# The second product of the second MLP with weights stationary, and its results turned on VectorE

## The chip, the cores and the metric

The kernel runs on one core of one Trainium2 chip. A core has TensorE (PE, whose weight loads are shown apart as PEld), VectorE (DVE), ScalarE (ACT), GpSimd (POOL), SyncE (SP, which here only issues DMAs) and 16 DMA engines. The metric is device time in microseconds, the median of some executions; smaller is better.

## The reference

Attention without softmax, then two MLPs one behind the other, all in float32:

```
scores = q @ k^T / 8, times gamma_h ** (i - j) where i >= j, else 0     # 4 x 8 heads, 576 tokens, 64 dims
x  = (scores @ v) as 2304 tokens x 512
h  = max(x @ w_in, 0);           x1  = (h * h) @ w_out                  # first MLP,  512 -> 2048 -> 512
h2 = x1 @ w_in2;  g = h2 * clip(h2 + 3, 0, 6) / 6;  out = g @ w_out2    # second MLP, 512 -> 2048 -> 512
```

The change touches only the last product, `g @ w_out2`, and the stores of `out`.

## The kernel before

Float32 products are made of three passes on rounded parts: an operand is split into a high part and a low part, and high x high, high x low and low x high are added up in PSUM. Attention and the first MLP come first and fill the span up to about 483 us; they write x1 to HBM. Meanwhile the second MLP's weights are narrowed, combined and split, and stored to HBM as `w_in_hl` and `w_out_hl`.

The second MLP then runs in three supers of 768 tokens. Each of its two products is done block-wise, with seven block products in place of eight: both operands are cut in 2 x 2 blocks, so a block has 384 tokens (`HALF`) and half of the features. `ORDER = (1, 6, 7, 5, 2, 4, 3)` is the order of the seven. In each super there are two stages:

- *First stage* (line 977): for each of 8 `j` and each of the 7 products, 6 matmuls with 128 columns of weights stationary and 384 tokens moving: 336 matmuls. ACT, DVE and POOL make the inputs `aop` of the second stage of what comes out.
- *Second stage* (lines 1017 to 1040): for each of the 7 products `q` and each of 8 `k`, the input is split by `a_cast` (ACT, line 921) and `a_low` (DVE, line 925) into one of 6 `spl` tiles. Then come 9 matmuls (line 1026): 128 tokens of `spl` stationary (3 groups), 256 columns of `w_out_hl` moving (`HALFD`), 3 passes. That is 504 matmuls. Two PSUM banks `z` hold the result of a product, tokens on partitions: two groups of tokens in one bank (512 wide), the third in the other (256 wide).

After products 1, 6 and 7, `merge` (lines 932 to 939) adds the banks to the running sums `held`. After products 5, 2, 4 and 3, `emit` (lines 941 to 953) makes output blocks in `tmp` tiles (four buffers), by DVE or, for product 2, by ACT, and SP stores each of the two pieces with one DMA, in runs of 256 floats (1 KB).

The weights of both stages come through a ring of 7 tiles of 512 KB (`ring_load`, lines 770 to 781): one tile serves two `k`. SP issues the load of tile n + 7 when PE has finished with tile n, so SP waits for PE before most ring loads. SP's queue is in order: a ring load behind a store waits until the store is issued. A store also waits until the DMA eight before it has landed, since eight semaphores are used in turn. A `tmp` tile is written again only when the store that read it has landed.

The order of the instructions on each engine is set when the program is built: a heap holds the work of ACT, DVE, POOL and SP with a due time (`at`), and `run(now)` issues what is due before the next group of matmuls. `t_in` and `t_out` are the planned times of a product in the first stage and in the second. An `spl` tile is planned to be written as soon as an older one is free.

Of the kernel before, what the change touches and what calls it, by code (L numbers as in the profile page):

```python
# [10 lines left out]
F32 = mybir.dt.float32  # L11
# [4 lines left out]
AF = mybir.ActivationFunctionType  # L16
ALU = mybir.AluOpType

P = 128
# [12 lines left out]


SUPERS, HALF = 3, 384
NTT = HALF // P
NJ = NF // 2
HALFD = DM // 2

# [55 lines left out]
def retention_moe_kernel(ctx: ExitStack, tc, qk, kv, w1, w2, cst, out):  # L94
# [5 lines left out]
    nc = tc.nc  # L100
    nblk = len(BLOCKS)
    start = np.concatenate([[0], np.cumsum([n for n, _ in BLOCKS])]).tolist()
# [658 lines left out]
    half = len(steps) - NJ  # L761
# [123 lines left out]
            at(t, ring_load, n)  # L885

    t_in = 6 * (HALF + 32) / 2400.0
    t_out = 3 * NJ * NTT * (HALFD + 32) / 2400.0
    now = 0.0
    act = nc.scalar.activation  # L890
    tt = nc.vector.tensor_tensor
# [32 lines left out]
        t = splits[s, q, k]  # L924
        tt(t[:, 1, :], f32(q, k), t[:, 0, :].bitcast(F32), ALU.subtract)  # L925

    PIECES = ((0, 2), (2, 1))

    def piece(t, n):
        return t[:, n * HALFD :] if n == 2 else t[:, : 2 * HALFD]  # L930

    def merge(q, o, u):

        for b, (n, m) in zip(A_BANKS[q], PIECES):
            p = z[b][:, : m * HALFD]
            if u is None:
                act(piece(o, n), p, AF.Copy, 0.0, SIXTH)
            else:
                stt(piece(o, n), p, SIXTH, piece(u, n), ALU.mult, ALU.add)

    def emit(s, q, half, od, u):
        for b, (n, m) in zip(A_BANKS[q], PIECES):
            t = tmpp.tile([P, 512], F32, tag="tmp", name=f"o_{s}_{q}_{n}")[:, : m * HALFD]
            p = z[b][:, : m * HALFD]
            if u is None:
                act(t, p, AF.Copy, 0.0, SIXTH)
            else:
                stt(t, p, SIXTH, piece(u, n), ALU.mult, ALU.add)
            t0 = (2 * s + half) * HALF + n * P
            dst = out[t0 : t0 + m * P, HALFD * od : HALFD * (od + 1)]  # L950
            nc.sync.dma_start(
                dst.rearrange("(n p) d -> p n d", p=P), t.rearrange("p (n d) -> p n d", n=m)
            )

    for s in range(SUPERS):
        t_a = now + NJ * 7 * t_in

        for m, (q, k) in enumerate((q, k) for q in ORDER for k in range(NJ)):
            free = t_a + (m - NSPL + 1) * t_out / NJ
            if m < NSPL:  # L960
                free = max(free, now + (k + 1) * 7 * t_in + 1.0)
            at(free + 0.1, a_cast, s, q, k)
            at(free + 0.7, a_low, s, q, k)
        for j in range(NJ):
            e = j % 2
            bank = {q: z[k][:, :HALF] for q, k in H_BANK[e].items()}
            s1, u2 = held[2 * e][:, 0, :], held[2 * e][:, 1, :]
            u3 = held[1][:, e, :]
            c22, c21, c12 = s1, u3, u2
            for i, q in enumerate(ORDER):  # L970
                run(now)
                w = wring[s, 0, j, i // 2][:, i % 2]
                x = x_ops[q]
                for k, (u, wi, xi) in enumerate(
                    [(u, wi, xi) for wi, xi in ((0, 0), (1, 0), (0, 1)) for u in range(2)]
                ):
                    nc.tensor.matmul(  # L977
                        bank[q],
                        w[:, wi, u * P : (u + 1) * P],
                        x[:, u, xi, :],  # L980
                        start=k == 0 and q not in (2, 4, 3),
                        stop=k == 5,
                        skip_group_check=q in (2, 4, 3),
                    )
                now += t_in
                if i % 2 or i == 6:
                    ring_done(now + 0.1)
                if q == 1:
                    at(now, act, s1, bank[1], AF.Copy)
                elif q == 6:  # L990
                    at(now, tt, u2, bank[6], s1, ALU.add)
                elif q == 7:
                    at(now, tt, u3, bank[7], u2, ALU.add)
                elif q == 5:
                    at(now, tt, c22, bank[5], u3, ALU.add)
                    at(now + 0.8, relu3, 4, j, c22)
                    at(now + 1.3, gate, 4, j, c22)
                elif q == 2:
                    at(now, relu3, 1, j, bank[1])
                    at(now + 0.75, gate, 1, j, bank[1])  # L1000
                elif q == 4:
                    at(now, tt, c21, bank[4], u2, ALU.add)
                    at(now + 0.8, relu3, 2, j, c21)
                    at(now + 1.3, gate, 2, j, c21)
                else:
                    at(now, tt, c12, bank[3], u2, ALU.add)
                    at(now + 0.8, relu3, 7, j, c12)
                    at(now + 1.3, gate, 7, j, c12)
                    at(now + 2.0, pool_op, 5, 7, 4, ALU.add, j)
                    at(now + 2.1, pool_op, 7, 1, 7, ALU.subtract, j)  # L1010
                    at(now + 2.2, pool_op, 6, 5, 1, ALU.subtract, j)
                    at(now + 2.3, pool_op, 3, 2, 6, ALU.subtract, j)
        if s + 1 < SUPERS:
            for u, st in enumerate(x_stages(s + 1)):
                for k, part in enumerate(st):
                    at(now + 1.0 + 25.0 * u * (k > 0) + 3.0 * k + 4.0 * (k > 0), do, part)
        s1, u3, u2 = [held[k].rearrange("p a b -> p (a b)")[:, : NTT * HALFD] for k in range(3)]
        for i, q in enumerate(ORDER):
            for k in range(NJ):
                run(now)  # L1020
                w, sp = wring[s, 1, q, k // 2], splits[s, q, k]
                for n in range(NTT):
                    rows = slice(P * n, P * (n + 1))
                    o = z[A_BANKS[q][n // 2]][:, HALFD * (n % 2) : HALFD * (n % 2 + 1)]
                    for m, (g, wi) in enumerate(((0, 0), (0, 1), (1, 0))):
                        nc.tensor.matmul(  # L1026
                            o,
                            sp[:, g, rows],
                            w[:, k % 2, wi, :],
                            start=k == 0 and m == 0 and n % 2 == 0 and q not in (2, 4, 3),  # L1030
                            stop=k == NJ - 1 and m == 2 and n > 0,
                            skip_group_check=q in (2, 4, 3),
                        )
                now += t_out / NJ
                if k % 2:
                    ring_done(now + 0.1)
            if q in (1, 6, 7):
                at(now, merge, q, *{1: (s1, None), 6: (u2, s1), 7: (u3, u2)}[q])
            else:
                at(now, emit, s, q, *{2: (0, 0, None), 5: (1, 1, u3), 4: (1, 0, u2), 3: (0, 1, u2)}[q])  # L1040
# [38 lines left out]
```

## Time and profile before

| | |
|---|---|
| time, median of 3 runs | 843.64 us (843.55 to 847.52) |
| the profiled execution's own time | 844.25 us |
| its span, first to last instruction | 842.4 us |
| PE busy | 823.3 us, 98% of the span |
| PEld busy | 758.6 us, 90% |
| DVE busy | 578.1 us, 69% |
| ACT busy | 385.7 us, 46% |
| POOL busy | 203.9 us, 24% |
| DMA packets | 136843, 185.79 MB, mean 221 GB/s |
| granted TensorE clock | 1.000 (2.4 GHz) |

Busy time is the time in which an engine had at least one instruction under way. The span leaves out what lies around the program: 844.25 - 842.4 = 1.85 us.

### The profile page before, as it was taken

The numbers are of one execution on the slowest core, as the hardware profiler recorded it, in microseconds if no ns is written. First come the engines' busy times: TensorE is split into PE (matmuls) and PEld (weight loads), VectorE is DVE, ScalarE is ACT, GpSimd is POOL, SyncE is SP. The second block draws the span as 40 slices with busy tenths as digits, with TensorE's granted clock in tenths as the row PEclk, the third lists the DMA queues.
The fourth block names the chain that finished last, engine by engine and source line by source line (L and its number), as shares of the span: only waits on it lengthen the run. The fifth ranks groups of instructions, "written<-read, shape, count | busy, mean of one in ns | idle before, by whom it ended". The sixth has DMA issues, their size and how long they took to land.

```text
span 842.4 us, 15782 instructions
## 1 busy us (share of the span) xinstructions
PE 823.3 (98%) x6052; PEld 758.6 (90%) x6052; DVE 578.1 (69%) x1034; ACT 385.7 (46%) x710; POOL 203.9 (24%) x182
## 2 busy tenths in 40 slices
PE   8899999998999999989999999999999999999998
PEld 7778779998888889989888899999999999999997
DVE  5788886565655556666546977887576987577763
ACT  1756644443434344434434633566333656234542
POOL 3366462001110101110000045520055500256300
PEclk9999999999999999999999999999999999999999
DMA  8927505666765457665547797788888978877773
GB/s 327 343 95 270 172 4 146 176 195 174 225 188 164 143 162 213 186 180 169 155 137 239 213 340 255 268 329 264 277 252 259 337 256 277 272 249 262 261 257 129
DMA packets 136843, 185.79 MB, mean 221 GB/s; under 512 B 7360, under 2 KB 94016, under 8 KB 136768
## 3 DMA queue, kind: packets, MB, share of 16 engines
q1 hardware_dynamic: 136768, 184.79, 68.7%
q8 instruction: 48, 0.79, 0.4%
q14 instruction: 27, 0.22, 0.1%
HBM read 145.96 MB, written 38.80 MB: 219 GB/s over the span
## 4 chain that ended last, share of the span: by engine, by line
PE 77%; DMA 6%; issue 5%; DVE 5%; POOL 3%; ACT 2%; SPq 2%; DVEq 0%; POOLq 0%; ACTq 0%
PE z L1026 21%; PE z L977 21%; PE acc L508 16%; PE h L472 16%; DMA w_in_hl<-seven 3%; POOL w L177 2%; DMA raw<-w_dram 1%; PE o L444 1%; PE o L434 1%; DVE r L482 1%; DMA w_out_hl<-seven 1%; ACT g L484 1%; DVE seven L568 1%; POOL q L333 1%; SPq L221 1%
## 5 line engine op out<-in xcount | busy, mean ns | idle before, releaser
L508 PE MATMUL acc<-g,w 128*128 128x512 f32 (+1 forms) x960 | 216.0, 373 | 3.0 <-ACT g L484 2.8
L472 PE MATMUL h<-x,w 128*128 128x512 f32 (+2 forms) x972 | 214.2, 368 | 4.5 <-ACT w L176 2.5
L472 PEld LDWEIGHTS h<-x,w 128*128 128x128 f32 x972 | 175.0, 188 | 31.7 <-ACT w L176 4.3
L508 PEld LDWEIGHTS acc<-g,w 128*128 128x128 f32 x960 | 173.5, 188 | 29.0 <-ACT g L484 3.5
L1026 PE MATMUL z<-ring,spl 128*128 128x256 f32 x1512 | 180.4, 282 | 0.0
L1026 PEld LDWEIGHTS z<-ring,spl 128*128 128x128 f32 x1512 | 180.3, 191 | 0.0
L911 POOL TENSOR_TENSOR aop<-aop,aop 128x384 f32<-128x384 f32 x96 | 107.5, 1131 | 294.7 <-DVE aop L908 184.7
L977 PE MATMUL z<-xop,ring 128*128 128x384 f32 x1008 | 175.6, 335 | 0.0
L977 PEld LDWEIGHTS z<-xop,ring 128*128 128x128 f32 x1008 | 175.1, 188 | 0.1
L925 DVE TENSOR_TENSOR spl<-aop,spl 128x384 fp32r<-128x384 f32 x168 | 99.3, 606 | 33.6 <-ACT spl L921 32.2
L921 ACT ACTIVATE spl<-aop 128x384 fp32r<-128x384 f32 x168 | 86.3, 522 | 59.9 <-PE z L1026 55.8
L482 DVE TENSOR_TENSOR r<-r,h 128x512 f32<-128x512 f32 (+1 forms) x80 | 50.5, 631 | 77.9 <-ACT r L481 77.3
L481 ACT ACTIVATE r<-h 128x512 f32<-128x512 f32 (+1 forms) x80 | 44.1, 552 | 122.3 <-PE h L472 120.5
L484 ACT ACTIVATE g<-r 128x512 fp32r<-128x512 f32 (+1 forms) x80 | 47.2, 589 | 107.3 <-DVE r L482 107.3
L905 ACT ACTIVATE aop<-held,con 128x384 f32<-128x384 f32 x72 | 44.5, 617 | 108.4 <-DVE held L872 107.8
L872 DVE TENSOR_TENSOR held<-z,held 128x384 f32<-128x384 f32 x120 | 66.5, 554 | 29.6 <-PE z L977 27.6
L490 DVE TENSOR_TENSOR g<-r,g 128x512 fp32r<-128x512 f32 (+1 forms) x80 | 54.9, 687 | 31.8 <-ACT g L484 31.8
L908 DVE SCALAR_TENSOR_TENSOR aop<-aop,held 128x384 f32<-128x384 f32 x72 | 49.7, 690 | 17.8 <-ACT aop L905 16.2
L177 POOL TENSOR_TENSOR w<-wt,w 128x512 fp32r<-128x512 f32 x32 | 43.0, 1348 | 51.6 <-ACT w L176 42.6
L339 POOL TENSOR_TENSOR kv<-kv,con 128x512 f32<-128x512 f32 x12 | 14.0, 1168 | 127.0 <-DMA kv<-kv_dram 109.3
L333 POOL TENSOR_TENSOR q<-q,con 128x512 f32<-128x512 f32 x13 | 19.4, 1494 | 99.1 <-issue 58.0
L567 DVE TENSOR_SCALAR seven<-uraw 128x512 int32<-128x512 int32 x32 | 15.7, 492 | 33.5 <-DMA w_in_hl<-seven 16.0
(80 smaller groups left out, 619.0 us busy)
## 6 DMA issues: line engine op xcount, KB each, us to landing
ring<-w_out_hl SPq DMA_DIRECT2D x84, 512.0 KB, 5.0
ring<-w_in_hl SPq DMA_DIRECT2D x72, 512.0 KB, 4.8
raw<-w_dram SPq DMA_DIRECT2D x32, 512.0 KB, 10.2
uraw<-w_dram SPq DMA_DIRECT2D x64, 256.0 KB, 3.4
q<-qk_dram SPq DMA_DIRECT2D x17, 512.0 KB, 6.3
kv<-kv_dram SPq DMA_DIRECT2D x30, 256.0 KB, 6.2
w_in_hl<-uhi SPq DMA_DIRECT2D x16, 448.0 KB, 4.4
w_in_hl<-seven SPq DMA_DIRECT2D x16, 448.0 KB, 4.2
```

Of the source, the lines that this page charges most:

```text
L177: nc.gpsimd.tensor_tensor(w[:, 1, :], t, w[:, 0, :].bitcast(F32), ALU.subtract)
L472: nc.tensor.matmul(hp[:, ts], w[:, wi, c * P : (c + 1) * P], x[:, xi, c, ts], start=k == 0, stop=k == 3 * NC - 1,)
L482: nc.vector.tensor_tensor(r, r, hp[:, :nb], ALU.mult)
L484: nc.scalar.activation(g[:, 0, :nb], r, AF.Copy)
L490: nc.vector.tensor_tensor(g[:, 1, :nb], r, g[:, 0, :nb].bitcast(F32), ALU.subtract)
L508: nc.tensor.matmul(acc[d][:, :nb], wt, g[:, gi, :nb], start=first, stop=stop)
L872: fn(*a)
L911: nc.gpsimd.tensor_tensor(f32(o, j), f32(a, j), f32(b, j), op)
L921: act(t[:, 0, :], f32(q, k), AF.Copy)
L925: tt(t[:, 1, :], f32(q, k), t[:, 0, :].bitcast(F32), ALU.subtract)
L977: nc.tensor.matmul(bank[q], w[:, wi, u * P : (u + 1) * P], x[:, u, xi, :], start=k == 0 and q not in (2, 4, 3), stop=k == 5, skip_group_ch ...
L1026: nc.tensor.matmul(o, sp[:, g, rows], w[:, k % 2, wi, :], start=k == 0 and m == 0 and n % 2 == 0 and q not in (2, 4, 3), stop=k == NJ - 1 ...
```

## The change

Before, tokens are stationary and weights move. After, in the second stage, 128 columns of weights are stationary (two groups `n`) and all 384 tokens of `spl` move: 6 matmuls for each `k`, 336 for a super. The result has output dims on partitions and tokens along the free axis, two banks of 384. `merge` and `emit` work on two pieces of 384 instead of one of 512 and one of 256. In `emit`, after the sum is made in a tile `o`, DVE turns it in blocks of 32x32 into a second tile `t` (`nc.vector.transpose`). In `t`, partition 32k + i and block b hold 32 output dims of token 32b + i. Four DMAs for each piece, one for each k, store 32 partitions x 12 blocks x 32 floats: runs of 128 bytes. So an `emit` issues 8 stores instead of 2, and uses 4 `tmp` tiles instead of 2.

```diff
@@ -32,7 +32,6 @@
 
 
 SUPERS, HALF = 3, 384
-NTT = HALF // P
 NJ = NF // 2
 HALFD = DM // 2
 
@@ -885,7 +884,7 @@
             at(t, ring_load, n)
 
     t_in = 6 * (HALF + 32) / 2400.0
-    t_out = 3 * NJ * NTT * (HALFD + 32) / 2400.0
+    t_out = 6 * NJ * (HALF + 32) / 2400.0
     now = 0.0
     act = nc.scalar.activation
     tt = nc.vector.tensor_tensor
@@ -924,33 +923,35 @@
         t = splits[s, q, k]
         tt(t[:, 1, :], f32(q, k), t[:, 0, :].bitcast(F32), ALU.subtract)
 
-    PIECES = ((0, 2), (2, 1))
-
-    def piece(t, n):
-        return t[:, n * HALFD :] if n == 2 else t[:, : 2 * HALFD]
-
     def merge(q, o, u):
 
-        for b, (n, m) in zip(A_BANKS[q], PIECES):
-            p = z[b][:, : m * HALFD]
+        for n, b in enumerate(A_BANKS[q]):
+            p = z[b][:, :HALF]
             if u is None:
-                act(piece(o, n), p, AF.Copy, 0.0, SIXTH)
+                act(o[:, n], p, AF.Copy, 0.0, SIXTH)
             else:
-                stt(piece(o, n), p, SIXTH, piece(u, n), ALU.mult, ALU.add)
+                stt(o[:, n], p, SIXTH, u[:, n], ALU.mult, ALU.add)
 
     def emit(s, q, half, od, u):
-        for b, (n, m) in zip(A_BANKS[q], PIECES):
-            t = tmpp.tile([P, 512], F32, tag="tmp", name=f"o_{s}_{q}_{n}")[:, : m * HALFD]
-            p = z[b][:, : m * HALFD]
+
+
+        t0 = (2 * s + half) * HALF
+        for n, b in enumerate(A_BANKS[q]):
+            t, r = (
+                tmpp.tile([P, 512], F32, tag="tmp", name=f"{x}_{s}_{q}_{n}")[:, :HALF] for x in "ot"
+            )
+            p = z[b][:, :HALF]
             if u is None:
                 act(t, p, AF.Copy, 0.0, SIXTH)
             else:
-                stt(t, p, SIXTH, piece(u, n), ALU.mult, ALU.add)
-            t0 = (2 * s + half) * HALF + n * P
-            dst = out[t0 : t0 + m * P, HALFD * od : HALFD * (od + 1)]
-            nc.sync.dma_start(
-                dst.rearrange("(n p) d -> p n d", p=P), t.rearrange("p (n d) -> p n d", n=m)
-            )
+                stt(t, p, SIXTH, u[:, n], ALU.mult, ALU.add)
+            nc.vector.transpose(r, t)
+            for k in range(P // 32):
+                d0 = HALFD * od + P * n + 32 * k
+                nc.sync.dma_start(
+                    out[t0 : t0 + HALF, d0 : d0 + 32].rearrange("(b i) d -> i b d", i=32),
+                    r[32 * k : 32 * k + 32].rearrange("i (b d) -> i b d", d=32),
+                )
 
     for s in range(SUPERS):
         t_a = now + NJ * 7 * t_in
@@ -1014,21 +1015,19 @@
             for u, st in enumerate(x_stages(s + 1)):
                 for k, part in enumerate(st):
                     at(now + 1.0 + 25.0 * u * (k > 0) + 3.0 * k + 4.0 * (k > 0), do, part)
-        s1, u3, u2 = [held[k].rearrange("p a b -> p (a b)")[:, : NTT * HALFD] for k in range(3)]
+        s1, u3, u2 = held
         for i, q in enumerate(ORDER):
             for k in range(NJ):
                 run(now)
                 w, sp = wring[s, 1, q, k // 2], splits[s, q, k]
-                for n in range(NTT):
-                    rows = slice(P * n, P * (n + 1))
-                    o = z[A_BANKS[q][n // 2]][:, HALFD * (n % 2) : HALFD * (n % 2 + 1)]
+                for n, b in enumerate(A_BANKS[q]):
                     for m, (g, wi) in enumerate(((0, 0), (0, 1), (1, 0))):
                         nc.tensor.matmul(
-                            o,
-                            sp[:, g, rows],
-                            w[:, k % 2, wi, :],
-                            start=k == 0 and m == 0 and n % 2 == 0 and q not in (2, 4, 3),
-                            stop=k == NJ - 1 and m == 2 and n > 0,
+                            z[b][:, :HALF],
+                            w[:, k % 2, wi, P * n : P * (n + 1)],
+                            sp[:, g, :],
+                            start=k == 0 and m == 0 and q not in (2, 4, 3),
+                            stop=k == NJ - 1 and m == 2,
                             skip_group_check=q in (2, 4, 3),
                         )
                 now += t_out / NJ
```

PE, the last three `k` of the last product (3) of the last super, before. `z` are the two PSUM banks, `ring` the weights, `spl` the split inputs; the first name behind the arrow is the moving operand's.

```order
L1026 MATMUL z_4742<-ring_8550,spl_3_5_8654 128x256 x6
L1026 MATMUL z_4743<-ring_8550,spl_3_5_8654 128x256 x3
L1026 MATMUL z_4742<-ring_8576,spl_3_6_8666 128x256 x6
L1026 MATMUL z_4743<-ring_8576,spl_3_6_8666 128x256 x3
L1026 MATMUL z_4742<-ring_8576,spl_3_7_8678 128x256 x6
L1026 MATMUL z_4743<-ring_8576,spl_3_7_8678 128x256 x3
```

The same place after:

```order
L1025 MATMUL z_4742<-spl_3_5_8281,ring_8191 128x384 x3
L1025 MATMUL z_4743<-spl_3_5_8281,ring_8191 128x384 x3
L1025 MATMUL z_4742<-spl_3_6_8290,ring_8211 128x384 x3
L1025 MATMUL z_4743<-spl_3_6_8290,ring_8211 128x384 x3
L1025 MATMUL z_4742<-spl_3_7_8299,ring_8211 128x384 x3
L1025 MATMUL z_4743<-spl_3_7_8299,ring_8211 128x384 x3
```

Nine matmuls of 256 columns for a `k` have become six of 384, three for each bank, and the operands have changed places.

DVE at the end of the program, the `emit` of products 4 (its last row) and 3, before:

```order
L948 SCALAR_TENSOR_TENSOR o_4_0_8639<-z_4740,held_4712 128x512
L948 SCALAR_TENSOR_TENSOR o_4_2_8642<-z_4741,held_4712 128x256
L925 TENSOR_TENSOR spl_3_5_8654<-aop_4719,spl_3_5_8654 128x384
L925 TENSOR_TENSOR spl_3_6_8666<-aop_4719,spl_3_6_8666 128x384
L925 TENSOR_TENSOR spl_3_7_8678<-aop_4719,spl_3_7_8678 128x384
L948 SCALAR_TENSOR_TENSOR o_3_0_8726<-z_4742,held_4712 128x512
L948 SCALAR_TENSOR_TENSOR o_3_2_8729<-z_4743,held_4712 128x256
```

and after:

```order
L948 STREAM_TRANSPOSE t_4_1_8268<-o_4_1_8267 128x384
L924 TENSOR_TENSOR spl_3_5_8281<-aop_4719,spl_3_5_8281 128x384
L924 TENSOR_TENSOR spl_3_6_8290<-aop_4719,spl_3_6_8290 128x384
L924 TENSOR_TENSOR spl_3_7_8299<-aop_4719,spl_3_7_8299 128x384
L947 SCALAR_TENSOR_TENSOR o_3_0_8332<-z_4742,held_4712 128x384
L948 STREAM_TRANSPOSE t_3_0_8333<-o_3_0_8332 128x384
L947 SCALAR_TENSOR_TENSOR o_3_1_8340<-z_4743,held_4712 128x384
L948 STREAM_TRANSPOSE t_3_1_8341<-o_3_1_8340 128x384
```

Each piece of an output is now followed by a STREAM_TRANSPOSE, which stands between the first piece's sum and the second's.

SP in the last super, around the `emit` of products 5 and 2, before:

```order
L780 DMA ring_8408<-w_out_hl 128x1024
L951 DMA out_dram<-o_5_0_8423 128x2x256
L951 DMA out_dram<-o_5_2_8426 128x256
L780 DMA ring_8440<-w_out_hl 128x1024
L780 DMA ring_8466<-w_out_hl 128x1024
L780 DMA ring_8492<-w_out_hl 128x1024
L780 DMA ring_8518<-w_out_hl 128x1024
L951 DMA out_dram<-o_2_0_8533 128x2x256
L951 DMA out_dram<-o_2_2_8536 128x256
```

and after:

```order
L779 DMA ring_8059<-w_out_hl 128x1024
L951 DMA out_dram<-t_5_0_8072 32x12x32 x4
L951 DMA out_dram<-t_5_1_8080 32x12x32 x4
L779 DMA ring_8095<-w_out_hl 128x1024
L779 DMA ring_8115<-w_out_hl 128x1024
L779 DMA ring_8135<-w_out_hl 128x1024
L779 DMA ring_8155<-w_out_hl 128x1024
L951 DMA out_dram<-t_2_0_8168 32x12x32 x4
L951 DMA out_dram<-t_2_1_8176 32x12x32 x4
```

Two stores have become eight in front of the same ring loads; they stand in the order of the two pieces.

## Rows read from the trace of the kernel before

**Rows 1.** First part of the page: busy us, share of the span, instructions.
```profile
span 842.4 us, 15782 instructions
PE 823.3 (98%) x6052; PEld 758.6 (90%) x6052; DVE 578.1 (69%) x1034; ACT 385.7 (46%) x710; POOL 203.9 (24%) x182
```
**Rows 2.** Chain that ended last, its end: start us, us, what, matmuls.
```profile
601.67 58.38 PE z L977 x336
660.05 59.99 PE z L1026 x504
720.03 58.35 PE z L977 x336
778.39 59.64 PE z L1026 x501
```
**Rows 3.** Windows, products 2, 4, 3 of the first super: length, busy by engine, clock, DMA.
```profile
core 0: us, PE busy (x) PEld busy (x) DVE busy (x) ACT busy (x) POOL busy (x), PEclk, DMA share, GB/s
575.96:584.53 8.57, 8.57 (x75) 8.57 (x74) 6.73 (x15) 5.98 (x13) 0.00 (x0) 1.00 0.85 273
584.53:593.10 8.57, 8.57 (x74) 8.57 (x74) 6.59 (x14) 5.76 (x14) 0.00 (x0) 1.00 0.88 292
593.10:601.67 8.57, 8.57 (x73) 8.57 (x72) 3.26 (x8) 1.56 (x3) 0.00 (x0) 1.00 0.84 274
```
**Rows 4.** Timeline of DVE at the first super's end: start us, us, what [idle before].
```profile
595.83 0.56 DVE L925 TENSOR_TENSOR spl<-aop,spl 128x384 fp32r<-128x384 f32 x1 [0.36 <-ACT spl L921]
601.35 1.02 DVE L948 SCALAR_TENSOR_TENSOR o<-z,held 128x512 f32<-128x512 f32 x2 [4.96 <-PE z L1026]
```
**Rows 5.** Groups by line and form, DVE: count | busy us, mean ns | idle before.
```profile
L174 DVE CAST w<-wt 128x512 fp32r<-128x512 f32 x14 | 16.0, 1145 | 0.5
L567 DVE TENSOR_SCALAR seven<-uraw 128x512 int32<-128x512 int32 x32 | 15.7, 492 | 33.5 <-DMA w_in_hl<-seven 16.0 <-DMA w_out_hl<-seven 10.1 <-ACT r L481 3.6
L659 DVE TENSOR_TENSOR xop<-xtop,xop 128x384 fp32r<-128x384 f32 x12 | 6.6, 550 | 0.0
```
**Rows 6.** Lines 221, 602, 780, 951, DMAs on SP: issue ns min/median/max, times; landing.
```profile
L221 SPq DMA_DIRECT2D kv<-kv_dram x28: 595/652/1288, 21.6 to 373.3; - x28
...
L602 SPq DMA_DIRECT2D w_out_hl<-uhi x16: 359/415/1197, 327.1 to 483.7; - x16
...
L780 SPq DMA_DIRECT2D ring<-w_out_hl x84: 319/320/1168, 531.3 to 823.4; - x84
DMA to landing us min/median/max: 3.8/5.0/8.8
...
L951 SPq DMA_DIRECT2D out_dram<-o x24: 378/404/429, 576.7 to 839.2; - x24
```
**Rows 7.** DMA view, window 404.1:407.1, in which packets have 512 bytes.
```profile
DMA packets 1523, 0.76 MB, mean 255 GB/s; under 512 B 33, under 2 KB 1523, under 8 KB 1523
q1 hardware_dynamic: 1523, 0.76, 86.8%
```
**Rows 8.** DMA view, window 317.33:317.43, eight 4-byte packets and one of 2 KB.
```profile
DMA packets 9, 0.00 MB, mean 21 GB/s; under 512 B 8, under 2 KB 8, under 8 KB 9
q1 hardware_dynamic: 9, 0.00, 9.6%
```
**Rows 9.** DMA view, window 13.9:24, in which packets have 4 KB.
```profile
DMA packets 1136, 4.13 MB, mean 409 GB/s; under 512 B 127, under 2 KB 127, under 8 KB 1136
q1 hardware_dynamic: 1136, 4.13, 102.0%
```
**Rows 10.** Timeline 815:842.4, the last stores.
```profile
821.52 0.90 SPq L951 DMA_DIRECT2D out_dram<-o  x2
830.44 9.23 SPq L951 DMA_DIRECT2D out_dram<-o  x4
838.05 1.02 DVE L948 SCALAR_TENSOR_TENSOR o<-z,held 128x512 f32<-128x512 f32 x2 [4.96 <-PE z L1026]
```
**Rows 11.** DMA view, window 838.8:842.4: busy tenths in 40 slices of 0.09 us.
```profile
DMA  0000000002799999999999510000000000000000
```

## The prediction

> **What bounds the kernel now.** Three views, in this order. The page's first part: PE is busy in 98% of the span, no other engine comes near it [rows 1]. Then the end of the chain of waits: the second MLP is six unbroken blocks of matmuls, and nothing but PE stands in them [rows 2]. A second stage takes 59.99 us for 504 matmuls, 119.0 ns each; a first stage, whose matmuls have 384 columns, takes 58.35 to 58.38 us for 336, 173.7 ns each. (The last block has three records fewer; at 59.99 us it ends at 778.39 + 59.99 = 838.38.) Then the windows of three products in a second stage: PE 8.57 of 8.57 us at full clock, 2.4 GHz, DVE 6.6 to 6.7 us in two of them, DMA share 0.84 to 0.88 [rows 3]. So PE sets the time, and the DMA engines are the next in line. Behind the last matmul come 842.4 - 838.38 = 4.02 us in which the last stores go out.
>
> **The change part by part.**
>
> *PE.* Both forms push the same columns: 504 x 256 = 336 x 384 = 129,024 for a stage. What differs is what each matmul costs beyond its columns. 256 columns take 106.7 ns at 2.4 GHz, so 12.3 ns go on top; 384 take 160.0, with 13.7 on top. 168 matmuls fewer pay that. The new form has the shape of the first stage (128x128 stationary, 384 moving), so I take its block: 58.37 us in place of 59.99, 1.62 us for a stage, **4.86 us for three**. The bounds are that block's (58.35 to 58.38), and no gain at all if it doesn't transfer (a rival below).
>
> *DVE.* Sums and merges stay even: 512 + 256 = 384 + 384 columns. New are 8 transposes for a super, 24 in all; the trace has none. On both sides: a one-input operation of 512 columns takes 492 ns, 384/512 of it is 0.37 us; the slowest, a cast of 512 columns, takes 1.145 us; a two-input operation of the same 128x384 takes 0.550 [rows 5]. I take 0.55, the same size. They stand in the stage, where products 2 and 4 leave DVE 8.57 - 6.73 = 1.84 and 1.98 us of idle time. With the product at 58.37 / 7 = 8.34 us and two transposes more, DVE has 7.8 us of work in it. What hides a burst is the lead of the splits: in the first super the last split is ready at 595.83 + 0.56 = 596.39 [rows 4], its matmuls start at about 601.67 - 1.07 = 600.60, 4.2 us later. So transposes cost PE nothing. At 1.145 us DVE would have 9.0 and 8.9 us in 8.34, 1.2 us too much over the two products, and a burst 1.2 us longer; both are inside 4.2 us. If that cover went, each microsecond of a late split would be one of PE.
>
> *SP.* An emit issues 8 stores for 2, 72 issues more in all. A store's issue takes 404 ns, two in a row 0.90 us [rows 6, 10]: 0.45 each, 3.6 us for an emit. Bounds: 0.32 (ring load) and 0.65 (the attention's stores to four-dimensional tiles, line 221) [rows 6]; a store of short runs with three dimensions as here, line 602, takes 0.415. Behind them in SP's queue stand ring loads: one that is due at a product's end is held back until about 4.3 us later (worked out with the tail). A ring tile that PE frees is wanted again 7 x 2.09 = 14.6 us later; less 5.0 us to landing [rows 6], 0.4 of issue and 4.3 of delay, 4.9 us are left. Cost to PE: none, as long as the DMA engines keep pace.
>
> *DMA.* An emit's data are 8 x 32 x 12 = 3,072 packets of 128 bytes, 192 on each of 16 engines. What such a packet takes no row shows. A 512-byte packet of a store took 0.868 x 3.0 us x 16 / 1523 = 27.4 ns [rows 7]; a 4-KB packet (1.02 x 10.1 x 16 - 1.1) / 1009 = 162 ns [rows 9]. On the line through these two (0.0376 ns for a byte) a 2-KB packet takes 85 ns, which leaves (0.096 x 0.10 us x 16 - 85 ns) / 8 = 9 ns for one of 4 bytes [rows 8]. So a 128-byte packet lies between 9 and 27 ns if size alone counts; the line between these ends gives 13.5, and I take that. An emit then keeps each engine busy for 2.6 us. The ring's four loads in a product are 32 packets of 4 KB on each engine, 5.2 us. 7.8 us in 8.34: full, but it fits, and the 4.9 us of lead take up what contention adds. At 27 ns it doesn't fit (rival A).
>
> *The tail.* Only the last emit lies on the end. Let E be the last matmul's end. Before: the first sum starts at 838.05, before E, since its bank is ready three matmuls (0.36 us) earlier; the stores are issued from 839.67 - 0.90 = 838.77 on [rows 10]; packets run from slice 9 to slice 23, 839.6 to 840.9 [rows 11], and 1.5 us later the program ends. So 0.85 us pass from an issue's start to its first packet. After: the first bank is ready 3 x 0.174 = 0.52 us before E, first sum E - 0.49 to E + 0.06, transpose to 0.61, second sum to 1.16, transpose to 1.71. Stores start at 0.66 and every 0.45 us; the eighth at 0.66 + 7 x 0.45 = 3.81, issued at 4.26. Its packets run from 4.66 for 24 x 13.5 ns = 0.3 us, and with 1.5 us the end is E + 6.5. That is **2.5 us more** than 4.02. With issues of 0.32 us it is 1.6 more, with 0.65 it is 3.9, with a transpose of 1.145 us 3.1.
>
> The Trainium skill, "DMA: Bandwidth & Descriptors", "Rules for kernel authors", advises to gather small transfers, since under 64 KB one pays mostly overhead. These stores of 48 KB go against it, and this trace agrees in kind: 1.5 us after the last packet and 0.85 before the first, whatever the size. If the eight paid it one behind the other, the tail would grow by 7 x (0.85 + 1.5 - 0.45) = 13 us more and the forecast be 854.6. The sum has it once: the two last stores of before are issued 0.45 us apart and their packets run without a gap [rows 10, 11], so they share it.
>
> *The sum*, against the profiled execution's 844.25 us: 844.25 - 4.86 + 2.5 = 841.9. The median of the runs is 0.61 us under that execution, so **841.3 us**, 2.4 us less than 843.64. By the bounds of issue the likeliest case runs from 843.64 - 4.86 + 1.6 = 840.4 to 843.64 - 4.86 + 3.9 = 842.7. A measurement of this kernel tells about 0.5%, 4.2 us, from no change; all of this is inside it.
>
> **The rivals.**
>
> *A, a short packet costs as much as one of 512 bytes; slower.* For it: the row of 27.4 ns is the shortest store in the trace. Against: the 4-byte packets take 9. Each product with an emit then has 192 x 27 ns = 5.2 + 5.2 = 10.4 us of DMA in 8.34; four of them leave 8.2 us, 4.9 of which the lead covers: PE waits 3.3 us in the first two supers, 6.6 together (in the last only six ring loads follow its first emit). The tail's packets run from 1.51 for 5.2 us, end E + 8.2, 4.2 more. 843.64 - 4.86 + 6.6 + 4.2 = 849.6. It decides from about 26 ns on, where the sum passes +4.2 us.
>
> *B, a store under 512 bytes costs a read and a write of its surroundings; much slower.* Two 512-byte packets: 55 ns, 10.6 us for an emit, 15.8 with the ring in 8.34. Four leave 29.7; less 4.9, PE waits 25 us in each of the first two supers. In the last, 42 us of stores and 8 of ring loads start 25 us before E, and the end is about 24 us later than now. 843.64 - 4.86 + 50 + 24 = 913. No store so short is in the trace, so nothing speaks for it there; the line from 4 KB down to 4 bytes speaks a little against it. The Trainium skill states this behaviour for transfers under 512 bytes ("DMA: Bandwidth & Descriptors", "Specifications"), without a price; no run here shows it.
>
> *C, PE gains nothing*, since the pace isn't set by the form alone: the stage stays at 59.99 us and the tail remains, 843.64 + 2.5 = 846.1. Against it: two blocks of the same shape at the same pace, with the same kinds of operands.
>
> *D, faster by over 0.5%.* The PE term is at most 4.9 us and the tail costs at least 1.6, so it needs something that the trace doesn't show.
>
> **How the numbers follow.** Forecast 0.60, C 0.06, A 0.16, B 0.13, D 0.05. Faster is D, 0.05. Same is the forecast and C, 0.66. Slower is A and B, 0.29. The range takes in the forecast's bounds, C and A: 840 to 850 holds 0.82.
>
> **What would show it.** In the profile after: second stages of 336 matmuls in about 58.4 us, without gaps; transposes of about 0.55 us; 36,864 packets under 512 bytes more, and a DMA share near 0.95 in the products with emits, while ring loads still land in 5 us or so; eight stores 0.45 us apart behind the last transposes, and 6.5 us from the last matmul to the end. Wrong would be matmuls that wait for ring loads, or DVE that waits for stores to land before it may write a `tmp` tile again: then the packets cost more than I took. Transposes above 2 us would make splits late.

## The result, and the profile after

The changed kernel takes 850.48 us (median of 5 runs, 849.54 to 853.96). The kernel before, run beside it on the same chip, takes 845.48 us. The ratio is 1.0069, with an interval of 1.0047 to 1.0092: slower by about 5.8 us. The forecast was 841.3 us in a range of 840 to 850, so the time lies above the range, and on the other side of no change.

The profile of after was taken of the slowest of its five executions, 853.96 us with a span of 851.8. It is 3.5 us above the median run; how much of that is waits is not shown. First its page: busy time, share of the span, instructions, as in [rows 1].

```profile
span 851.8 us, 14909 instructions
PE 821.6 (96%) x5548; PEld 754.6 (89%) x5548; DVE 592.4 (70%) x1058; ACT 385.7 (45%) x710; POOL 203.6 (24%) x182
```

The span is 9.4 us longer and PE busy 1.7 us less: PE waits. The chain of waits shows where (start us, us, what), the answer to [rows 2]:

```profile
484.84 58.37 PE z L978 x336
543.21 49.66 PE z L1025 x287
592.87 4.85 DMA ring<-w_out_hl
...
597.86 4.40 PE z L1025 x24
602.26 4.18 PE z L978 x24
...
611.45 4.01 DMA ring<-w_in_hl
...
615.60 47.15 PE z L978 x270
662.74 40.63 PE z L1025 x234
...
719.99 1.73 SPq L951
...
721.77 1.52 SPq L951
...
723.90 4.04 DMA ring<-w_in_hl
...
728.07 5.31 PE z L978 x30
733.38 4.12 DMA ring<-w_in_hl
...
737.63 48.69 PE z L978 x270
786.32 57.84 PE z L1025 x333
```

Before, the six stages stood there without a break. Now stores (line 951, `SPq`), ring loads behind them, and matmuls that wait for these loads take turns. Three undisturbed matters can be read first. The second stage of the last super, 57.84 us with three records missing, is 58.36 us for 336: the forecast's 58.37. The first stage ahead of all stores is 58.37. And the ring loads in the chain land 4.0 to 4.85 us after their issue, no later than before (5.0 in [rows 6]). Over the whole run the medians are 4.8 and 4.9 us (lines 777 and 779). They don't land slowly; they are issued late.

From one stage's start in the chain to the next (543.21, 602.26, 662.74, 722.35, 786.32; where the chain leaves PE, at 722.35, it is the end of the stage's last matmul, and PE's last one ends at 844.67) the stages take 58.37, 59.05, 60.48, 59.61, 63.97 and 58.35 us. Above 58.37 that is 9.6 us. The view of PE's waits has 6.7 of it (us in total, times, longest):

```profile
PE z L978 <- DMA ring<-w_in_hl: 5.2, 4, 2.0
PE z L1025 <- DMA ring<-w_out_hl: 1.5, 2, 1.0
```

Some 1.7 us more are the clock. In the windows around the longest wait (737.63) PEclk, behind the busy times, falls to 0.74 and 0.83 in 4 us each: some of these matmuls ran at 1.2 in place of 2.4 GHz. (1 - 0.74) x 4 + (1 - 0.83) x 4 = 1.7.

```profile
717.00:737.00 20.00, 16.14 (x90) 15.55 (x90) 9.62 (x19) 3.91 (x7) 3.48 (x4) 1.00 0.84 229
737.00:741.00 4.00, 3.37 (x14) 3.40 (x15) 1.74 (x3) 0.58 (x1) 0.51 (x1) 0.74 1.05 389
741.00:745.00 4.00, 4.00 (x22) 4.00 (x21) 2.13 (x5) 1.62 (x3) 0.53 (x1) 0.83 1.05 390
745.00:750.00 5.00, 5.00 (x30) 5.00 (x30) 3.41 (x6) 1.09 (x2) 3.48 (x4) 1.00 0.79 249
```

What is left, 9.6 - 6.7 - 1.7 = 1.2 us, goes for the most part with the six waits too: a matmul lasts 0.335 us in the mean and the next starts 0.174 us after it, so they overlap by 0.16 us, and each wait gives that up. 6 x 0.16 = 1.0 us, an estimate.

In the same rows the DMA share is 0.84 while PE waits, and 1.05 at 390 GB/s as soon as the held-back loads are out.

SP's own timeline in the first super shows who holds them back (start us, us, what):

```profile
578.82 3.96 SPq L951 DMA_DIRECT2D out_dram<-t  x8
582.89 1.85 SPq L779 DMA_DIRECT2D ring<-w_out_hl  x4
585.54 7.23 SPq L951 DMA_DIRECT2D out_dram<-t  x8
592.87 0.90 SPq L779 DMA_DIRECT2D ring<-w_out_hl  x2
593.85 0.90 SPq L777 DMA_DIRECT2D ring<-w_in_hl  x2
594.84 7.71 SPq L951 DMA_DIRECT2D out_dram<-t  x8
602.65 1.93 SPq L777 DMA_DIRECT2D ring<-w_in_hl  x4
604.68 6.67 SPq L951 DMA_DIRECT2D out_dram<-t  x8
611.45 17.26 SPq L777 DMA_DIRECT2D ring<-w_in_hl  x14
```

The first eight stores take 3.96 us, as forecast for an emit (3.6 and a little). The next three emits, each behind a burst of ring loads, take 7.23, 7.71 and 6.67. From 585.54 to 611.45 SP has no pause: 9.30 and 9.84 us from one emit to the next, while a product lasts 8.34. For these products SP's queue is the bound, and the backlog grows until PE misses a tile. In the second super the emits take 4.74, 7.35, 9.21 and 7.35 us.

The DMA engines are not idle while SP is held: in the three long holds above, with the ring loads issued just ahead of them still under way, their share is 0.98, 0.95 and 1.02 (1.00, 0.82 and 0.91 in the second super). They run half empty at the end of a hold and behind it, 0.51 from 591.50 to 594.00 and 0.65 from 601.50 to 604.70, because the next loads have only just been issued. So engine time goes lost around the ends of the holds.

The single issues (line 951: ns min/median/max) say how:

```profile
L951 SPq DMA_DIRECT2D out_dram<-t x96: 316/478/2077, 578.8 to 848.9; - x96
```

The median is the 0.45 us of the forecast, but the longest takes 2.08 us; before, it was 0.429 [rows 6]. In the emit at 594.84 the eight issues alone add up to 7.33 of its 7.71 us.

The other new work is as it was taken. The transposes (line 948), and the DMA view of the window 846:851, in which only the last stores run:

```profile
L948 DVE STREAM_TRANSPOSE t<-o x24: 578/578/581, 578.2 to 845.8; 128x384 f32<-128x384 f32 x24
```

```profile
DMA  0168716871588238842885178616861687200000
DMA packets 3200, 0.39 MB, mean 79 GB/s; under 512 B 3200, under 2 KB 3200, under 8 KB 3200
q1 hardware_dynamic: 3200, 0.39, 49.8%
```

A packet takes 0.498 x 5 us x 16 / 3200 = 12.5 ns (13.5 forecast). The busy tenths rise and fall eight times, once for each store: the engines wait for SP's issues, not the other way round.

The tail, from the last matmul (844.67) to the end (851.82), is 7.15 us in place of 4.02, and 6.5 were forecast. Its rows, the answer to [rows 10] (start us, us, what):

```profile
844.77 0.58 DVE L948 STREAM_TRANSPOSE t<-o 128x384 f32<-128x384 f32 x1
845.38 3.96 SPq L951 DMA_DIRECT2D out_dram<-t  x8
845.83 0.58 DVE L948 STREAM_TRANSPOSE t<-o 128x384 f32<-128x384 f32 x1
```

All in all, against the span of before: 842.4 + 1.5 (the second MLP starts at 484.84 in place of 601.67 - 59.99 - 58.37 = 483.31 [rows 2], which the change doesn't touch) - 3 x 1.62 + 9.6 + 3.1 = 851.7 (851.8).

### The profile page after: what moved, and what is told of

Read it like the earlier page. It is cut to its first block, busy times and chain, and to the rows that moved or that the text cites. A ratio compares the mean times of both kernels' runs of the same rounds, so it can differ in the third digit from the quotient of the medians.

```text
span 851.8 us, 14909 instructions
## 1 busy us (share of the span) xinstructions
PE 821.6 (96%) x5548; PEld 754.6 (89%) x5548; DVE 592.4 (70%) x1058; ACT 385.7 (45%) x710; POOL 203.6 (24%) x182
## 4 chain that ended last, share of the span: by engine, by line
PE 71%; DMA 11%; DVE 7%; issue 4%; SPq 3%; POOL 2%; ACT 2%; DVEq 0%; POOLq 0%; ACTq 0%
PE z L978 19%; PE z L1025 18%; PE acc L507 16%; PE h L471 15%; DMA w_out_hl<-seven 3%; DMA raw<-w_dram 2%; DMA kv<-kv_dram 2%; DMA w_in_hl<-seven 2%; DMA ring<-w_in_hl 1%; SPq L951 1%; POOL w L176 1%; PE o L443 1%; DVE r L481 1%; PE o L433 1%; ACT g L483 1%
## 5 line engine op out<-in xcount | busy, mean ns | idle before, releaser
L978 PE MATMUL z<-xop,ring 128*128 128x384 f32 x1008 | 178.1, 337 | 5.2 <-DMA ring<-w_in_hl 5.2
L1025 PE MATMUL z<-spl,ring 128*128 128x384 f32 x1008 | 176.0, 335 | 1.5 <-DMA ring<-w_out_hl 1.5
L1025 PEld LDWEIGHTS z<-spl,ring 128*128 128x128 f32 x1008 | 175.0, 188 | 2.1 <-issue 2.1
```

What stands on the lines that cost most here:

```text
L978: nc.tensor.matmul(bank[q], w[:, wi, u * P : (u + 1) * P], x[:, u, xi, :], start=k == 0 and q not in (2, 4, 3), stop=k == 5, skip_group_ch ...
L1025: nc.tensor.matmul(z[b][:, :HALF], w[:, k % 2, wi, P * n : P * (n + 1)], sp[:, g, :], start=k == 0 and m == 0 and q not in (2, 4, 3), stop ...
```

## The experiments

All were timed in five rounds against the kernel before. The theory that came out of the profile is called Q in the expectations: PE waits because eight stores in a row hold SP's in-order queue, so that ring loads go out late. Its rivals put the loss on the packets of 128 bytes and the traffic itself, or on DVE and the transposes; the letters that the expectations use for them belong to these. "Wait" is what PE waits for ring tiles in the second MLP, "hold" the time from the first store's issue to the last one's end in an emit of the first two supers.

| kernel | stores of an emit | ratio to before, interval | wait us | tail us | hold us |
|---|---|---|---|---|---|
| before | 2, runs of 1 KB | 1 | 0 | 4.0 | 0.9 |
| after | 8, 128 B | 1.0069 [1.0047, 1.0092] | 6.7 | 7.15 | 4.0 to 9.2 |
| e4 | 2, 1.5 KB, not turned | 0.9919 [0.9890, 0.9948] | 0 | 3.6 | under 1 |
| e6 | 2, 1.5 KB, turned | 0.9921 [0.9898, 0.9944] | 0 | 4.7 | 0.9 to 1.7 |
| e1 | 8, 1.5 KB, turned | 1.0026 [1.0008, 1.0043] | 2.8 | 6.6 | 3.6 to 7.1 |
| e2 | 8, 128 B, from POOL | 1.0012 [0.9988, 1.0035] | 0 | 9.3 | none on SP |
| e3 | 8, 128 B, spread out | 0.9973 [0.9956, 0.9989] | 0 | 7.5 | one at a time |
| e5 | old products, 6, 128 B | 1.0024 [1.0004, 1.0044] | 0 | 6.6 | 3.2 to 6.0 |
| e9 | as after, 8 ring tiles | 1.0006 [0.9993, 1.0019] | 0.8 | 7.2 | 4.0 to 8.3 |
| e10 | as after, 6 ring tiles | 1.0168 [1.0141, 1.0194] | 11.1 | 7.1 | 4.0 to 7.7 |
| e7 | 4, 256 B | 0.9957 [0.9938, 0.9975] | 0 | 6.5 | 1.9 to 2.3 |
| e8 | as e7, two queues at the end | 0.9958 [0.9943, 0.9974] | 0 | 6.5 | as e7 |

**The matmuls alone (e4).** The new matmuls, without transposes, and each sum stored by one DMA:

```diff
-            nc.vector.transpose(r, t)
-            for k in range(P // 32):
-                ...
+            e = ((s * 2 + half) * 2 + od) * 2 + n
+            flat = out.rearrange("t d -> (t d)")[e * P * HALF : (e + 1) * P * HALF]
+            nc.sync.dma_start(flat.rearrange("(i x) -> i x", i=P), t)
```

> The new matmuls, sums and merges alone: no transposes, and two stores per output block of 128 partitions in runs of 1536 bytes; the output's layout is not the reference's. All theories: the three second stages take 58.5 us as in the first stage, 4.9 us saved, the tail as before or 0.3 us shorter: 840.5, ratio 0.994. If it is 845 instead, the matmuls do not bring the gain.

Measured 839.01 us. All six stages take 58.5 us from first start to last end (58.37 from one start to the next), and PE waits for nothing: the gain on PE is whole. The ratio is 1.8 us better than 0.994. In the one profile the second MLP starts at 481.2 us, 1.9 earlier than in that of before; over all profiles of this study it starts between 481.2 and 486.1. What moves this start wasn't looked into.

**With the transposes (e6).** As e4, but with `nc.vector.transpose(r, t)` and `r` stored.

> The changed kernel with its transposes, but two stores per output block of 128 partitions in runs of 1536 bytes (the output's layout is not the reference's): what the transposes alone cost, beside the fourth experiment, which had none. Q: no PE waits, only the tail is longer by two transposes, 1.16 us: ratio 0.9933 to 0.9955. If transposes hurt (splits late, or tile waits), PE waits show in the second stage and the ratio is 0.998 or more.

Measured 839.27 us, no wait, stages of 58.5 us, a tail of 4.72 us. Against e4's 3.58 the tail is 1.14 longer, which is two transposes (2 x 0.578). Inside the stages 24 transposes cost nothing, as the forecast had it.

**Eight stores of long runs (e1).** As after, but each store writes one run of 1536 bytes for each partition: 32 packets of 1536 bytes in place of 384 of 128, the same bytes.

```diff
-                    out[t0 : t0 + HALF, d0 : d0 + 32].rearrange("(b i) d -> i b d", i=32),
-                    r[32 * k : 32 * k + 32].rearrange("i (b d) -> i b d", d=32),
+                flat = out.rearrange("t d -> (t d)")[e * 32 * HALF : (e + 1) * 32 * HALF]
+                nc.sync.dma_start(flat.rearrange("(i x) -> i x", i=32), r[32 * k : 32 * k + 32])
```

> The changed kernel with its eight stores per output block kept, each of 32 partitions, but every partition's 384 floats go out as one run of 1536 bytes (32 packets per store in place of 384); the output's layout is not the reference's. Theory Q (SP's queue: short-run stores keep SP in their issue while many packets are outstanding, and ring loads stand behind them): issues come back to 0.4 to 0.5 us each, no PE waits, 845.5 - 4.9 + 2 = 842.6, ratio 0.997. Theory E (the DMA engines' time for short packets delays the ring's data): 842.6 too, since the packets' time falls from 2.6 to about 1 us per output block. Theory N (the number of stores alone): as the changed kernel, 850, ratio 1.006.

Measured 847.43 us: the 0.997 that I had given for Q was a miss. The short runs are not the whole cause; eight issues in a row are bad enough. SP's waits show a second brake, the one that the kernel's description has: a store waits until the DMA eight before it has landed (what waits for what: us in total, times, longest; then PE's waits):

```profile
SPq L952 <- DMA ring<-w_in_hl: 10.4, 9, 1.8
SPq L952 <- DMA ring<-w_out_hl: 10.4, 12, 1.7
```

```profile
PE z L976 <- DMA ring<-w_in_hl: 2.8, 4, 1.1
```

The last four stores of an emit wait for the four ring loads that were issued ahead of the emit. In e1 the eight issues add up to 2.9 to 3.5 us of holds of 6.2 to 7.1; the rest are these waits. In after the view lists no such wait for a store (one gap of 0.34 us, at 732.11, ends behind a landing), and the issues themselves are long. But there, too, each of the last four stores starts behind the landing of its load: in the emit at 585.54 the loads land at 587.13, 588.40, 589.73 and 591.04, and the stores start at 588.14, 588.73, 590.85 and 591.37. So in after one brake may hide the other.

**The stores on another engine (e2).** `nc.gpsimd.dma_start` in place of `nc.sync.dma_start`, no other edit.

> The changed kernel with the same 128-byte-run stores issued by POOL, which is nearly idle in the second stage; SP issues ring loads alone. Q: the ring loads are on time again, no PE waits for them, 842 to 844, ratio 0.997 (if POOL's issue itself is slow, only the tail grows). E: the same packets on the same engines, PE waits about 4.8 us as now, 850, ratio 1.006.

Measured 845.53 us. PE's waits are gone, all six stages at 58.5 us. That fits Q, but it doesn't decide against E, because the traffic isn't the same: the bytes are, but the page shows the stores on a queue of their own, in 3,072 packets (half of them of 3 KB, half of 4 bytes) in place of 36,864 of 128 bytes:

```profile
q0 software_dynamic: 3072, 4.72, 2.2%
```

That is 0.022 x 842.7 us / 96 = 0.19 us of each engine for a store; 24 packets of 12.5 ns are 0.30. And the tail grows to 9.3 us and eats the gain. The last eight issues on POOL, and the times of an issue there (ns min/median/max) and to its landing:

```profile
834.36 4.87 POOL L951 DMA_DIRECT2D out_dram<-t  x8 [2.94 <-DVE t L948]
```

```profile
L951 POOL DMA_DIRECT2D out_dram<-t x96: 615/617/782, 577.5 to 838.6; - x96
...
DMA to landing us min/median/max: 2.0/4.2/5.4
```

**The same stores, spread (e3).** SP issues them, one after each `k` of the next product, ring loads in between:

```diff
-                nc.sync.dma_start(
+                at(
+                    when + 1.3 + 0.95 * (4 * n + k),
+                    nc.sync.dma_start,
```

> The changed kernel with the eight stores of an output block spread over the next product, one for each k, so that at most two or three stand in front of a ring load on SP; same packets, same engines, same queue. Q: a ring load is held back by at most some 2 to 3 us, no PE waits, 843, ratio 0.997. E: 849 to 850, ratio 1.005, since the engines have the same work.

Measured 843.98 us, 0.9973, as Q had it. PE waits for nothing. Queue, stores, packets and bytes are those of after; only the order on SP differs. Issues are still long at times, up to 1.57 us (316 to 2077 in after), but a ring load stands behind one to three of them, not behind eight:

```profile
L871 SPq DMA_DIRECT2D out_dram<-t x96: 315/464/1574, 578.4 to 839.1; - x96
```

The window 585:611, with three emits, tells the traffic from the order. After, then e3 (columns as in [rows 3]):

```profile
585.00:611.00 26.00, 25.36 (x145) 24.78 (x144) 18.51 (x37) 9.91 (x20) 0.00 (x0) 1.00 0.93 267
585.00:611.00 26.00, 26.00 (x151) 26.00 (x151) 18.79 (x38) 10.37 (x21) 0.64 (x1) 1.00 1.04 289
```

In e3 the DMA engines carry more in the same time, 289 GB/s in place of 267, and PE doesn't wait. (The share adds up the times of packets, so it can pass 1.) This is the run that decides against E.

**Short stores in the old kernel (e5).** The kernel before, with six stores for an emit in place of two, each of 512 runs of 128 bytes: the same 3,072 packets.

```diff
-            dst = out[t0 : t0 + m * P, HALFD * od : HALFD * (od + 1)]
-            nc.sync.dma_start(...)
+            for g in range(m):
+                dst = out[t0 + g * P : t0 + (g + 1) * P, HALFD * od : HALFD * (od + 1)]
+                for a in range(2):
+                    nc.sync.dma_start(dst.rearrange("p (b a f) -> p b a f", a=2, f=32)[:, :, a], ...)
```

> The kernel before, with its old matmuls and no transposes, but its stores cut into runs of 128 bytes: six stores per output block in place of two, 3072 packets per block as in the changed kernel (128 partitions x 4 runs each; the columns stand in a wrong order in the output). Theory Q (stores in a row hold SP, ring loads stand behind them, PE waits): PE waits for ring loads here too, some 2 to 7 us, and the tail grows by about 2: 849 to 854, ratio 1.005 to 1.010. Theory M (the new matmuls need the ring earlier or run uneven, the stores alone do nothing): only the tail, 847.5, ratio 1.0025.

Measured 847.99 us. Q's 1.005 to 1.010 was a miss, the rival's 1.0025 was met, for a reason that Q allows: six stores hold SP for 3.2 to 6.0 us, and with 7 ring tiles PE waited, in these runs, only where holds were above some 6 us. Single issues took up to 2.30 us. What is left is the tail, 6.6 in place of 4.0. So the packets by themselves cost the stages next to nothing here (one stage of six was 0.3 us longer), though with six stores and products of 8.57 us this is a milder test than after.

**One ring tile more, one fewer (e9, e10).** `RING = 8` (with `NSPL = 5`, to make room) and `RING = 6` in the changed kernel.

> The changed kernel with 8 ring tiles instead of 7 (and 5 tiles for the split inputs instead of 6, to make room). Stores, issues and bytes are unchanged; a ring load may be 8 x 2.09 - 7 x 2.09 = 2.09 us later before PE misses it. Theory Q (PE waits because the loads behind eight stores go out late): the longest wait in the changed kernel was 2.02 us, so all waits vanish or fall under 0.3 us, second stages take 58.5 us, the 6.5 us of waits and the 1.7 us of low clock come back, the tail stays at about 7 us: ratio to the kernel before 0.998 (0.996 to 1.000). Rival T (the DMA engines can't carry stores and loads in that time, so a deficit builds up whatever the lead): a tile more puts the waits off but doesn't take them away, ratio 1.003 to 1.008. Rival S: with 5 split tiles the splits come late and PE waits for spl instead of ring.

> The changed kernel with 6 ring tiles instead of 7: 2.09 us less lead, nothing else. Theory Q: the eight blocks of the first two supers that held SP for 4 to 9.2 us all make PE wait, each 1 to 2 us longer than now where there was a wait (5 of them, 6.5 us in all), and for the first time where the hold was 4.7 to 6: 6.5 + 8 x 1.5 = some 18 us of waits for ring tiles, ratio 1.018 (1.012 to 1.028, with the clock falling more often). Rival T (engines too busy): the deficit is set by bytes and packets, not by the lead, the waits grow by at most 2.09 us for each super, ratio 1.007 to 1.012.

Measured 845.80 and 859.62 us. With 8 tiles SP is held as long as in after, 4.0 to 8.3 us, but one wait is left; with 6 tiles there are nine for ring tiles. PE's waits of e9, then of e10:

```profile
PE z L978 <- DMA ring<-w_in_hl: 0.8, 1, 0.8
```

```profile
PE z L1025 <- DMA ring<-w_out_hl: 5.6, 5, 1.8
PE z L978 <- DMA ring<-w_in_hl: 5.5, 4, 2.2
```

e9 ends just above the 0.996 to 1.000 expected of Q, since 0.8 us of wait stayed and the stages lost 2.1 us in all; 2.1 - 4.9 + 3.1 is its ratio. PE has no wait for `spl` in it, so rival S is out. e10's is inside Q's range, with 11.1 us of waits for ring tiles where some 18 were expected. Its stages take 17 us more than 58.5 each: to these waits come one of 1.3 us for ACT ahead of all stores, and the lower clock (0.66 in the 4 us from 741 on, behind a wait of 2.2 us). Rival T's ranges, 1.003 to 1.008 and 1.007 to 1.012, were both missed. A lead of 2.09 us more or less decides, at the same traffic: the loss is one of when the loads go out.

**Half as many stores (e7).** The columns of `w_out2` are dealt so that the two pieces of an emit hold alternate groups of 32 output dims. Both are turned into one tile, which comes from another pool (`xpre`) than the `tmp` tiles, and four DMAs for an emit store runs of 256 bytes. `out` has the reference's layout.

```diff
+        tag = "top0" if q in (5, 4) else "low0"
+        r = xpre.tile([P, HALF // 32, 2, 32], F32, tag=tag, name=f"t_{s}_{q}")
         for n, b in enumerate(A_BANKS[q]):
             ...
-            nc.vector.transpose(r, t)
+            nc.vector.transpose(r[:, :, n, :], t.rearrange("p (b d) -> p b d", d=32))
+        for k in range(P // 32):
+            d0 = HALFD * od + 64 * k
+            nc.sync.dma_start(
+                out[t0 : t0 + HALF, d0 : d0 + 64].rearrange("(b i) d -> i b d", i=32),
+                r[32 * k : 32 * k + 32].rearrange("i b e d -> i b (e d)"),
+            )
...
+    w_out2 = np.asarray(inputs["moe2_w_out"]).reshape(DFF, 2, 4, 2, 32)
+    w_out2 = w_out2.transpose(0, 1, 3, 2, 4).reshape(DFF, DM)
```

> The changed kernel with the weights' columns dealt so that both pieces of a block can be turned into one tile, in runs of 256 bytes: four stores per output block in place of eight, 1536 packets in place of 3072, all else as in the changed kernel. Q: four stores hold SP for about 2 us and are no more than the four ring loads between them, so no or little PE waiting, tail +2 against before: 843.0 of 845.3, ratio 0.995 to 0.998. Theory P (any short run is enough to hold the queue): 1.002 or more, with PE waits of over 2 us.

Measured 842.03 us, 0.9957 [0.9938, 0.9975]: faster than both kernels. SP at the place of the timeline of after (start us, us, what):

```profile
578.83 1.92 SPq L951 DMA_DIRECT2D out_dram<-t  x4
580.85 1.88 SPq L779 DMA_DIRECT2D ring<-w_out_hl  x4
585.01 2.17 SPq L951 DMA_DIRECT2D out_dram<-t  x4
587.28 1.00 SPq L779 DMA_DIRECT2D ring<-w_out_hl  x2
```

Four stores hold it for about 2 us, and it has pauses again (2.3 us from 582.73 to 585.01). All stages take 58.5 us. What remains of the price is the tail.

**The last stores on two queues (e8).** As e7, but ACT issues every other one of the last emit's four stores.

```diff
-            nc.sync.dma_start(
+            (nc.scalar if s == SUPERS - 1 and q == 3 and k % 2 else nc.sync).dma_start(
```

> The seventh experiment's kernel with the last output block's four stores issued by SP and ACT in turn, the rest as there. The tail ends about 0.9 to 1 us earlier than in the seventh (two issues less in a row), elsewhere nothing changes: ratio 0.994 to 0.997.

Measured 842.13 us, with a tail of 6.48 us as in e7: a miss. The issues do end 1.0 us earlier after the last matmul (2.7 in place of 3.7 us). The DMA views of 833:843, of e7 and then of e8 (last matmul at 833.92 and 836.41), show why that gives nothing:

```profile
DMA  0000000000000079998999940000000000000000
```

```profile
DMA  9920000000000000000000008999899993000000
...
q10 hardware_dynamic: 800, 0.20, 12.0%
```

From the first store on the engines are full, for 2.5 us in both. A packet of 256 bytes takes 0.12 x 10 us x 16 / 800 = 24 ns; 96 of them on each engine are 2.3 us. In after (12.5 ns, 192 packets) the issues set the tail's pace; here the packets do. The Trainium skill, "DMA: Bandwidth & Descriptors", "Rules for kernel authors", says that spreading DMAs over issuing engines saves only issue time, since all run on the same 16 DMA engines; these rows agree.

## Why the prediction was wrong

- *PE, 1.62 us for a stage*: right. Undisturbed stages took 58.36 and 58.37 us, and in e2, e3, e4, e6, e7 and e8 all three second stages had the forecast's length. The form of a matmul set its price, whoever is stationary; rival C is out.
- *DVE*: right. A transpose took 0.578 us (0.55 taken) and was hidden; two of them stand in the tail (e6 against e4).
- *DMA*: the packet was right, 12.5 ns for 13.5. Rival A's 850 is near the time measured, but its reason, packets of 27 ns, did not occur, nor did B's 55. The Trainium skill, "DMA: Bandwidth & Descriptors", "Specifications", has transfers under 512 bytes read and written back; if these did so, a packet's 12.5 ns doesn't show it, and e3 with all of them beats before.
- *SP*: here it failed, in "0.45 each, 3.6 us for an emit" and with it in "Cost to PE: none". The median issue was 0.48 us, but the price was taken from two stores in a row, and multiplied by eight. With eight in a row behind ring loads that are still under way, an issue takes up to 2.1 us (after) or a store waits for the DMA eight before it (e1), and the eight hold SP for 6.7 to 9.2 us in six of the first eight emits. (Line 221, from which the upper bound of 0.65 came, issues loads of k and v, not stores.) The description of the kernel names that wait; the sum left it out. With the forecast's own lead (14.6 - 5.0 - 0.4 us), a load that is held back for 9.2 + 0.7 us in place of 4.3 comes 0.7 us late, and SP can't keep up with products of 8.34 us. e3, e9 and e10 show this without a change in the traffic. e3, which only mends the order, has a ratio of 0.9973; the forecast was 841.3 / 843.64 = 0.9972, in part by luck, since e3's tail is 1 us longer than forecast.
- *"Full, but it fits"* was right of the DMA engines (e3: share 1.04 and no wait), though fuller than the 7.8 of 8.34 us forecast. It looked at them and not at the queue that feeds them: in after they were nearly full while SP was held (0.95 to 1.02 in the first super, 0.82 in the longest hold) and half empty behind it (0.51, 0.65).
- *The sign of being wrong*, matmuls that wait for ring loads, came. The reason given with it, that the packets cost more than taken, did not hold.
- *The tail*: 3.1 us more in place of 2.5; the eight issues took 0.50 us each, 0.4 more, and the last packet came 1.5 us after its issue's start in place of 1.15.
- *Not in the sum*: the clock, 1.7 us in the profiled execution, which follows the longest wait, and some 1 us for the overlap of matmuls that six waits gave up.

What stays open is what the long issues would cost without the waits for landings (e1 shows the reverse, those waits with short issues and long runs: 2.8 us of PE waits), why an issue gets long behind loads under way, and what moves the start of the second MLP.

## What to carry to other kernels

Where loads that an engine needs stand behind stores in one in-order queue, count the queue's time for a period as one would an engine's, with issues at the price they have while other DMAs are under way, and with the waits for the DMAs that hold the semaphores; it must be less than the period. To cut one store into many is then dearer than its packets: deal the data so that few stores remain (e7), or put the loads between the stores (e3). A gain of 0.6% on the bound engine is lost to a few waits of 1 to 2 us, and the end of the program pays for each step that is added between the last result and its store.

## What the runs showed of the hardware

- An issue on SP took 316 to 2077 ns for the same form of store (32 partitions, 12 runs of 128 bytes), and up to 2302 ns for stores of 512 runs (e5). On POOL the issues of the same stores took 615 to 782 ns. They landed after 4.2 us in the median, from SP after 2.9 (after) and 4.6 us (e3).
- A packet of 128 bytes took 12.5 ns, one of 256 bytes 24 ns and one of 512 bytes 27.4 [rows 7]: four times 128 bytes are dearer than 512, twice are not dearer than 256.
- Behind a wait of 2.0 us on PE the granted clock was 0.74 and then 0.83 in two stretches of 4 us (after), behind one of 2.2 us it was 0.66 and 0.91 (e10). Behind one of 1.55 us, at 728.07 in after, it stayed at 1.00. The two longer waits thus cost more than they lasted.
